# DeltaNet and channel mixer on one core: one block substitution for both units of batch 0, with a new order of the work

## The chip, the cores and the metric

The program runs on one core of one Trainium2 chip. Its time is the device time of one launch in microseconds (us); the kernel before takes 618.48 us, the median of 3 runs (618.42 to 619.09). A core has five engines with queues of their own: TensorE (PE, with its weight loads shown as PEld), VectorE (DVE), ScalarE (ACT), GpSimd (POOL) and SyncE (SP). Each works through its queue in the order in which the program emitted it, and semaphores make an instruction wait for another engine.

## The reference

Four batches, eight heads, 768 tokens, 48 channels per head; then a channel mixer over 384 channels with a low-rank token mix of rank 32.

```python
def _attn_ref(q, k, v, beta) -> np.ndarray:
    B, H, S, D = q.shape
    k_n = k / (np.linalg.norm(k, axis=-1, keepdims=True) + 1e-06)
    state = np.zeros((B, H, D, D), dtype=np.float32)
    y = np.zeros_like(q)
    for t in range(S):
        kt, vt, bt = (k_n[:, :, t], v[:, :, t], beta[:, :, t, None])
        y[:, :, t] = np.einsum('bhd,bhde->bhe', q[:, :, t], state)
        v_old = np.einsum('bhde,bhd->bhe', state, kt)
        state = state + bt[:, :, :, None] * np.einsum('bhd,bhe->bhde', kt, vt - v_old)
    return y.astype(np.float32)
...
def _moe_ref(x, U, V, w_ch1, w_ch2) -> np.ndarray:
    xt = x.transpose(0, 2, 1)
    h = xt @ U @ V
    u = x + h.transpose(0, 2, 1)
    ch = np.maximum(u @ w_ch1, 0.0) @ w_ch2
    return (u + ch).astype(np.float32)
```

The weights `U`, `V`, `w_ch1` and `w_ch2` arrive as 64-bit floats and are turned into 32-bit ones on the chip, in integer and float operations.

## The kernel before

**The recurrence in chunks.** Each batch's 768 tokens are cut into 12 chunks of 64. Six chunks of all eight heads form a unit, so there are eight units, two to a batch (`SPLIT = (0, 1)` are those of batch 0). For each unit the kernel

1. loads k, q, v and a second copy of k (`load`, L513; names "k", "q", "v", "z") over SP's and POOL's queues;
2. transposes k and q on TensorE (`turn`, L646 or L420, copied out by ScalarE at L660 or, for the first, L655 and L657) and multiplies them in `products` (L673). The 32 x 32 diagonal blocks of the k products go to `diag` (ScalarE L683, VectorE L686), the whole to `pg` (L693), for units 0 and 1 also to half of `hs` (`alone`, L697); the q products are masked into `qk` by VectorE (L704);
3. lays the diagonal blocks out for VectorE in `gs`, one block per partition, by a 32 x 32 transpose (L749), takes the norms of k from their diagonals (`norms`, L593 to L618) and puts the factor beta/norm^2 on the diagonal of `xt`, which POOL has zeroed (L743);
4. inverts the triangular blocks by substitution: VectorE scales `gs` (L753) and then does one multiplication (L758, into `prod`) and one subtraction (L764, into `xt`) per step. For units 0 to 2 each 32 x 32 block is taken as two 16 x 16 blocks side by side (15 steps), for the others whole (31 steps);
5. transposes the result back into `zz` (L771), joins the 16 x 16 halves on TensorE where a unit was split (`joins`, L780 to L837, with `part` at L790 writing to `S1` and `S2`), and the 32 x 32 blocks into 64 x 64 ones (L854 to L885); `diagonals` (L893, L900) puts the blocks in place in `pg`.

There is one `gs`, one `xt` and one `zz`. So unit n is laid out when unit n-1 is substituted, and returned to `zz` when unit n-1 is joined.

**The recurrence.** `recur` runs over the 12 chunks of a batch. `prepare` (L973, L984, copied out at L992 and L997) makes ready three chunks at a time from a joined half of a unit. Each chunk then needs a product with the state (L1022), a subtraction on VectorE (L1035), the state's update (L1050, added at L1060) and the outputs (L937, L951), which ScalarE copies to `X` (L921).

**The weights.** `load_weights` fetches 14 slices: 0 is U, 1 is V, 2 to 7 are `w_ch1`, 8 to 13 are `w_ch2`. Each is converted by VectorE in five operations (L1155 to L1183), with one of ScalarE (L1140) between. The slices land in three rooms in turn: the half of `X` that batch 1 uses later, `wide`, and the first half of `hs`.

**The mixer.** `front` does the low-rank token mix and transposes its result into `ut` (L1346 to L1390), 256 tokens at a time, three groups to a batch. `channels` is the first layer (L1447, six pairs of tiles for each group, with ReLU at L1412), `narrow` the second (L1562), done with seven products on sums and differences of halves (`add_up`, `sums`); VectorE adds its results to `X` (L1487). Batch 3 uses such sums for its first layer too (`quick`, L1251). `channels`, `narrow`, `front` and `turn` have a second form in which a product is split into quarters of the array (L408, L420); it is taken while other quartered work is running, where the list of places allows it with the word `quad`.

**What sets the order.** The work is written as generators, and a planner in the program (`run`, L341) interleaves them before anything runs on the chip. Each yield is a need (keys that other parts have emitted) or an operation with engine and assumed cost. Of the operations that could start about as soon, the one with the lowest rank goes first. Ranks come from the list `PLACES` (L142 to L258), by name of the part and its indices; a part that isn't listed has the default given at `begin`. The planner only fixes the order in each engine's queue; the waits between engines follow from which tile is written and read where.

Of the kernel before, what the change touches and what calls it, by code (L numbers as in the profile page):

```python
# [8 lines left out]
FP32 = mybir.dt.float32  # L9
# [7 lines left out]
BK = 32  # L17
# [9 lines left out]
def kernel(  # L27
# [115 lines left out]
    add_up b0 i0 76.06; add_up b0 i1 10; add_up b0 i2 92; add_up b1 i0 94.5; add_up b1 i1 -57.95  # L143
    add_up b1 i2 13.5; add_up b2 i0 4.89; add_up b3 i0 119.12; add_up b3 i1 17.69; add_up b3 i2 2.95
    blocks n1 83.63; blocks n2 19.95; blocks n3 96.74; blocks n4 107.02; blocks n5 204.56; blocks n6 121.16
    blocks n7 126.66; both 73; channels b0 i0 e0 96.95; channels b0 i0 e1 105.6; channels b0 i0 e2 -27.57
    channels b0 i0 e3 129.38; channels b0 i0 e4 91.95; channels b0 i0 e5 71.15; channels b0 i1 e0 25
    channels b0 i1 e1 19.03; channels b0 i1 e2 34; channels b0 i1 e3 5.2; channels b0 i1 e4 84.16
    channels b0 i1 e5 30.5; channels b0 i2 e0 52; channels b0 i2 e1 46.94; channels b0 i2 e2 75.56
    channels b0 i2 e3 116.36; channels b0 i2 e4 51.09; channels b0 i2 e5 99.28; channels b1 i0 e0 113.65  # L150
    channels b1 i0 e1 91.5; channels b1 i0 e2 53.98; channels b1 i0 e3 100.61; channels b1 i0 e5 120.34
    channels b1 i1 e0 128.05; channels b1 i1 e1 30.85; channels b1 i1 e2 104.15; channels b1 i1 e3 58.65
    channels b1 i1 e4 15.5; channels b1 i1 e5 91.65; channels b1 i2 e0 118.43; channels b1 i2 e1 -2.08
    channels b1 i2 e2 73.28; channels b1 i2 e3 -8.98; channels b1 i2 e4 111.65; channels b1 i2 e5 32.87
    channels b2 i0 e0 38.24; channels b2 i0 e2 4.5; channels b2 i0 e3 127.92; channels b2 i0 e4 22.75
    channels b2 i0 e5 95.78; channels b2 i1 e0 274.53; channels b2 i1 e1 94; channels b2 i1 e2 97.16
    channels b2 i1 e3 91.59; channels b2 i1 e4 73; channels b2 i1 e5 1.09; channels b2 i2 e0 28.09
    channels b2 i2 e1 44.19; channels b2 i2 e2 57.06; channels b2 i2 e3 68.5; channels b2 i2 e4 73
    channels b2 i2 e5 9.5; copies 56.49; cut 75.73; diagonals n0 h0 19.22; diagonals n0 h1 62.5
    diagonals n1 h0 52; diagonals n2 h0 15.5; diagonals n2 h1 94.5; diagonals n3 h0 32; diagonals n3 h1 93.24  # L160
    diagonals n4 h0 7.5; diagonals n4 h1 95.58; diagonals n5 h0 33.96; diagonals n5 h1 27; diagonals n6 h0 92.63
    diagonals n6 h1 -0.5; diagonals n7 h0 88.94; diagonals n7 h1 69.62; first 30.4; front b0 i0 -7.49
    front b0 i0 quad 1; front b0 i1 75.5; front b0 i1 quad 1; front b0 i2 -10.38; front b1 i0 71.77
    front b1 i1 76; front b1 i1 quad 1; front b1 i2 73.06; front b2 i0 4.43; front b2 i0 quad 1; front b2 i1 12.82
    front b2 i1 quad 1; front b2 i2 68.32; front b2 i2 quad 1; front b3 i1 -1.47; front b3 i2 94.5
    gather b0 i0 h0 c0 77.72; gather b0 i0 h0 c1 16.74; gather b0 i0 h1 c0 -15; gather b0 i1 h0 c0 -18.11
    gather b0 i1 h0 c1 -19.16; gather b0 i1 h1 c0 111.34; gather b0 i1 h1 c1 99.53; gather b0 i2 h0 c0 109.5
    gather b0 i2 h0 c1 36.92; gather b0 i2 h1 c0 4.78; gather b0 i2 h1 c1 84.78; gather b1 i0 h0 c0 21.21
    gather b1 i0 h1 c0 79.5; gather b1 i0 h1 c1 103.91; gather b1 i1 h0 c0 92.5; gather b1 i1 h0 c1 122.8
    gather b1 i1 h1 c0 101.5; gather b1 i2 h1 c0 77.08; gather b1 i2 h1 c1 45; gather b2 i0 h0 c0 13.32  # L170
    gather b2 i0 h0 c1 82.99; gather b2 i0 h1 c0 124.83; gather b2 i0 h1 c1 3.53; gather b2 i1 h0 c0 80.62
    gather b2 i1 h0 c1 73.95; gather b2 i1 h1 c0 80.36; gather b2 i1 h1 c1 76.58; gather b2 i2 h0 c0 95.84
    gather b2 i2 h1 c0 25.35; gather b3 i0 h0 c0 2.88; gather b3 i0 h0 c1 113; gather b3 i0 h1 c1 113
    gather b3 i1 h0 c0 -4; gather b3 i1 h0 c1 23.12; gather b3 i1 h1 c0 44.69; gather b3 i1 h1 c1 28.1
    gather b3 i2 h0 c0 105.1; gather b3 i2 h0 c1 37.88; gather b3 i2 h1 c0 109.03; gather b3 i2 h1 c1 92.38
    grams n0 i0 54.5; grams n0 i1 5; grams n1 i0 -5.73; grams n1 i1 16.5; grams n2 i0 64.85; grams n2 i1 5.5
    grams n3 i0 10.25; grams n4 i0 140.55; grams n4 i1 0; grams n6 i1 103.46; grams n7 i0 120.26
    grams n7 i1 124.04; joins n0 h1 42; joins n1 h0 -10.78; joins n1 h1 90.6; joins n2 h0 46.2; joins n2 h1 -9.38
    joins n3 h0 18.36; joins n3 h1 -3; joins n4 h0 49.57; joins n4 h1 108.36; joins n5 h0 6.33; joins n5 h1 -4.95
    joins n6 h1 102.05; joins n7 h0 91.09; joins n7 h1 -26.22; last_sum b0 i0 107.65; last_sum b0 i1 -0.5  # L180
    last_sum b0 i2 58; last_sum b1 i0 6.24; last_sum b1 i1 90.99; last_sum b1 i2 72.32; last_sum b2 i0 -3.27
    last_sum b2 i1 94.5; last_sum b3 i1 76.04; last_sum b3 i2 90; load n0 namek halves(0,) -2.13
    load n0 namek halves(1,) 6.19; load n0 nameq halves(0,) 89.12; load n0 nameq halves(1,) 77.79
    load n0 namev halves(0,) 106; load n0 namez halves(0,) 113.97; load n0 namez halves(1,) 7.5
    load n1 namek halves(0,) 81.07; load n1 namek halves(1,) 73.91; load n1 nameq halves(0,) 43.57
    load n1 nameq halves(1,) 91.1; load n1 namev halves(0,) 27.89; load n1 namev halves(1,) 70.76
    load n1 namez halves(0,) 93.39; load n1 namez halves(1,) 5.01; load n2 namek halves(0, 1) 29.55
    load n2 nameq halves(0, 1) 67.61; load n2 namev halves(0, 1) 60.56; load n2 namez halves(0, 1) 107.23
    load n3 namek halves(0, 1) 11; load n3 nameq halves(0, 1) -4.84; load n3 namev halves(0, 1) 66.59
    load n3 namez halves(0, 1) 25.89; load n4 namek halves(0, 1) 65.35; load n4 nameq halves(0, 1) 24.5  # L190
    load n4 namev halves(0, 1) 81; load n4 namez halves(0, 1) 30.74; load n5 namek halves(0, 1) 109.5
    load n5 nameq halves(0, 1) 92; load n5 namev halves(0, 1) 38.85; load n5 namez halves(0, 1) -21.49
    load n6 namek halves(0, 1) 32.5; load n6 nameq halves(0, 1) 37.61; load n6 namev halves(0, 1) 7.15
# [388 lines left out]
    def landed(name, n, j=1):  # L582
        return need(*[(name, n, g, j) for g in range(2)])

    def norms(n):

        _, _, _, _, _, vn, _, _ = units[n]
        b, hf = divmod(n, NU)
# [1052 lines left out]
```

## Time and profile before

| what | value |
| --- | --- |
| median of 3 runs | 618.48 us (618.42 to 619.09) |
| span of the profiled execution | 612.3 us |
| PE busy | 582.1 us (95%) |
| PEld busy | 502.3 us (82%) |
| DVE busy | 417.3 us (68%) in 1000 instructions |
| ACT busy | 236.6 us (39%) |
| POOL busy | 98.4 us (16%) |
| first L1447 (first layer of the mixer) | 119.84 us |
| first L1562 (second layer) | 143.0 us |
| shares of the chain that ended last | PE 83%, DVE 11%, issue 2%, ACT 2% |

The span counts from the first to the last instruction of one profiled execution; the runs are timed from outside it, so their median is 6.2 us longer. Busy times are those of the engine's own instructions, without waits. A stretch's clock is the share of full speed that TensorE was granted in it.

### The profile page before, as it was taken

To read this page: it belongs to the slowest core of one execution; us is meant where nothing else is said; L and a number is where in the kernel's file an instruction comes from. 1 tells how busy PE (TensorE), PEld (TensorE's weight loads), DVE (VectorE), ACT (ScalarE), POOL (GpSimd) and SP (SyncE) were. 2 spreads that over 40 slices of the span, in tenths; PEclk is the share of its full clock that TensorE was granted. 3 is DMA by queue.
4 is the path that set the end of the run, shared out by engine and by line. 5 is a ranking of instruction groups with operands and counts; after the bars stand their busy time and mean duration, and the time that the engine had idled before them with its cause. 6 is when DMAs were issued, how large, how long until landed. Compare 5 with 4: busy or idle time off the path is not lost.

```text
span 612.3 us, 24053 instructions
## 1 busy us (share of the span) xinstructions
PE 582.1 (95%) x10824; PEld 502.3 (82%) x10824; DVE 417.3 (68%) x1000; ACT 236.6 (39%) x466; POOL 98.4 (16%) x169
## 2 busy tenths in 40 slices
PE   4798887999999999999999999999999999999997
PEld 4788786688989987988889988978989889656997
DVE  5998899898899348988895888287843223332542
ACT  3645666255412652265218224253163220344000
POOL 8321050520004304110043002220010000000000
PEclk9655557799999999999999999999999999999999
DMA  9911686940006205200071002310000000000000
GB/s 142 163 42 55 209 193 169 137 130 19 3 28 98 67 4 91 61 16 3 4 123 42 16 16 53 74 42 4 28 3 3 29 2 1 26 2 0 16 36 27
DMA packets 63847, 33.31 MB, mean 54 GB/s; under 512 B 50816, under 2 KB 61824, under 8 KB 63744
## 3 DMA queue, kind: packets, MB, share of 16 engines
q1 hardware_dynamic: 56800, 23.21, 17.6%
q0 software_dynamic: 5344, 8.27, 6.5%
q8 instruction: 85, 1.39, 0.9%
q10 hardware_dynamic: 1600, 0.30, 0.3%
q14 instruction: 18, 0.15, 0.1%
HBM read 27.03 MB, written 4.72 MB: 52 GB/s over the span
## 4 chain that ended last, share of the span: by engine, by line
PE 83%; DVE 11%; issue 2%; ACT 2%; POOL 1%; DMA 1%; DVEq 0%; ACTq 0%; POOLq 0%
PE P L1562 25%; PE P L1447 24%; PE P L1251 7%; PE P L673 3%; PE P L408 3%; PE P L1364 2%; PE P L646 2%; PE P L1022 2%; PE P L973 2%; PE P L1050 2%; PE P L984 2%; PE P L951 2%; DVE prod L758 2%; PE P L937 2%; DVE xt L764 2%
## 5 line engine op out<-in xcount | busy, mean ns | idle before, releaser
L1447 PE MATMUL P<-ut,w_sb 128*128 128x256 f32 x648 | 151.6, 385 | 0.1
L1447 PEld LDWEIGHTS P<-ut,w_sb 128*128 128x128 f32 x648 | 119.4, 190 | 18.2 <-issue 1.2
L1562 PE MATMUL P<-w_sb,hs 128*128 128x192 f32 x468 | 82.4, 330 | 0.2 <-ACT hs L1412 0.2
L1562 PEld LDWEIGHTS P<-w_sb,hs 128*128 128x128 f32 x468 | 75.9, 190 | 2.0 <-ACT hs L1412 0.3
L764 DVE TENSOR_TENSOR xt<-xt,prod 128x112 f32<-128x112 f32 (+21 forms) x200 | 64.6, 323 | 6.9
L758 DVE TENSOR_TENSOR prod<-gs,xt 128x112 f32<-128x112 f32 (+21 forms) x200 | 64.0, 320 | 4.4
L1487 DVE TENSOR_TENSOR X<-X,P 128x192 f32<-128x192 f32 x84 | 29.3, 351 | 53.5 <-PE P L1562 50.7
L1412 ACT ACTIVATE hs<-P 128x512 f32<-128x512 f32 x54 | 32.3, 597 | 82.9 <-PE P L1447 73.6
L921 ACT COPY X<-P 64x192 f32<-64x192 f32 x96 | 30.0, 313 | 80.7 <-PE P L951 74.0
L1562 PE MATMUL P<-w_sb,S 128*128 128x192 f32 x264 | 45.9, 328 | 0.0
L1562 PEld LDWEIGHTS P<-w_sb,S 128*128 128x128 f32 x264 | 42.9, 190 | 1.2 <-DVE X L1487 0.6
L531 POOL DMA_DIRECT2D slot<-in_k_dram x44 | 29.1, 671 | 64.3 <-PE P L1050 64.2
L646 PE MATMUL P<-ident,slot 128*128 128x128 f32 x192 | 30.8, 309 | 8.2 <-DMA slot<-in_k_dram 8.1
L673 PE MATMUL P<-slot 48*64 48x64 f32 x1536 | 32.8, 243 | 4.8 <-ACT slot L660 4.8
L893 ACT COPY slot<-zz 32x384 f32<-32x384 f32 x64 | 32.5, 508 | 9.1 <-DVE zz L832 4.9
L673 PEld LDWEIGHTS P<-slot 48*64 48x64 f32 x1536 | 29.4, 155 | 7.9 <-ACT slot L660 6.0
L646 PEld LDWEIGHTS P<-ident,slot 128*128 128x128 f32 x192 | 25.0, 158 | 11.7 <-issue 8.7
L1251 PE MATMUL P<-slot,w_sb 128*128 128x384 f32 x96 | 33.2, 486 | 0.0
L1562 PE MATMUL P<-w_sb,slot 128*128 128x192 f32 x180 | 30.6, 327 | 0.9 <-DVE X L1487 0.9
L660 ACT COPY slot<-P 128x768 f32<-128x768 f32 x30 | 23.5, 796 | 20.1 <-PE P L646 18.0
L1562 PEld LDWEIGHTS P<-w_sb,slot 128*128 128x128 f32 x180 | 29.4, 190 | 2.0 <-DVE X L1487 1.5
L531 POOL DMA_DIRECT2D slot<-in_q_dram x32 | 21.0, 664 | 56.8 <-ACT X L921 40.5
(150 smaller groups left out, 935.9 us busy)
## 6 DMA issues: line engine op xcount, KB each, us to landing
out_dram<-X SPq DMA_DIRECT2D x22, 192.0 KB, 1.9
X<-in_moe_w_ch_dram SPq DMA_DIRECT2D x10, 384.0 KB, 3.9
wide<-in_moe_w_ch_dram SPq DMA_DIRECT2D x10, 384.0 KB, 4.4
slot<-in_k_dram SPq DMA_DIRECT2D x48, 72.0 KB, 4.8
slot<-in_k_dram POOLq DMA_DIRECT2D x44, 72.0 KB, 4.8
slot<-in_q_dram SPq DMA_DIRECT2D x32, 72.0 KB, 4.4
slot<-in_q_dram POOLq DMA_DIRECT2D x32, 72.0 KB, 4.7
slot<-in_v_dram SPq DMA_DIRECT2D x32, 72.0 KB, 3.4
```

Source lines behind the costliest of these rows:

```text
L531: queue.dma_start(out=t[half(1 - g if name == "z" else g), :, to, 0:D], in_=src[b, 4 * g + s, hf * UC * L : (hf + 1) * UC * L, :].rearrang ...
L646: nc.tensor.transpose(p_t[:, c // 3, c % 3], t[:, c, 2 * j : 2 * j + 2].rearrange("p s d -> p (s d)"), ident,)
L673: nc.tensor.matmul(p_g[half(g ^ (par * i)), par, c], kq[rows, c, j, 0, half(g)], kq[rows, c, j, i, half(g)], start=True, stop=True,)
L758: nc.vector.tensor_tensor(out=prod, in0=gb[:, :, j : j + 1, j + 1 :].to_broadcast([128, split, m, w]), in1=xb[:, :, 0:m, j : j + 1].to_bro ...
L764: nc.vector.tensor_tensor(out=xb[:, :, 0:m, j + 1 :], in0=xb[:, :, 0:m, j + 1 :], in1=prod, op=ALU.subtract,)
L893: nc.scalar.copy(pg[quarter(i), :, at, :, a : a + BK], cut(zc, h)[quarter(i)].rearrange("p r (c j) t -> p r c j t", j=2),)
L921: nc.scalar.copy(x[half(c % 2), c // 2, 4 * D * g : 4 * D * (g + 1)].rearrange("p (j r d) -> p r j d", r=2, d=D), states(p_y)[half(g)],)
L1251: nc.tensor.matmul(to, w, t, start=start, stop=stop, skip_group_check=True)
L1412: nc.scalar.activation(hs[:, fs[0] : fs[1] + 1 : fs[1] - fs[0]], p_f, ACTF.Relu)
L1447: nc.tensor.matmul(p_f[:, x], w(x, t), ut[:, t], start=(t == 0), stop=(t == KT - 1))
L1487: nc.vector.tensor_tensor(out=to, in0=to, in1=p, op=ALU.add)
L1562: nc.tensor.matmul(to, of[0], of[1], start=of[2], stop=of[3], skip_group_check=True)
```

## The change

Units 0 and 1 no longer take turns in `gs`, `xt` and `zz`. Each gets its own matrices in `w2_sb`, the room of the second layer's weights, which is filled later: `matrices` returns, for units 0 and 1, a part of `gs_first`, of `xt_first` and of the rest of that room; the other units keep the old tiles. One substitution then runs over both, with the four 16 x 16 blocks of a partition (two per unit) in each operation: 15 steps for both units in place of 15 each. The norms of both are taken together as 64 columns, and POOL zeroes both matrices in one instruction. `blocks` is cut into `lay`, `substitution`, `back` and `rest`; `lay` and `back` are parts with ranks of their own.

```diff
+    def matrices(n):
+
+        if n in SPLIT:
+            at = slice(MS * n, MS * n + MS)
+            return gs_first[:, at], xt_first[:, at], first[:, 4 * MS :][:, ZZ * n : ZZ * n + ZZ]
+        return gs.rearrange("p s t -> p (s t)"), xt.rearrange("p s t -> p (s t)"), zz
...
+    def norms(n, many=1):
...
+        yield need(("seeded", n), ("scaled", n - 2), *[("laid", n + y) for y in range(many)])
...
+    def lay(n):
+        diag = units[n][6]
+        yield need(*[("diag", n, j) for j in range(2)], *[("substituted", n - 1)] * (n >= NU))
         yield op("dve", 2.0)
+        nc.vector.transpose(squares(matrices(n)[0]), diag.rearrange("p q t -> p t q"))
+        emitted(("laid", n))
+
+    def back(n):
+        yield need(("substituted", n), *[("joined", n - 1)] * (n > NU))
+        yield op("dve", 2.0)
+        _, x, z = matrices(n)
         nc.vector.transpose(
+            z[:, 0 : BK * BK].rearrange("p (q t) -> p t q", t=BK),
+            squares(x).rearrange("p s t -> p t s"),
         )
         emitted(("returned", n), 0.1)
+        yield from rest(n)
+
+    def first_blocks():
+
+        def seed():
+            yield op("pool", 2.1)
+            nc.gpsimd.memset(xt_first, 0.0)
+            emitted(("seeded", 0), 0.1)
+
+        begin(seed(), place_of(0))
+        for n in SPLIT:
+            begin(lay(n), place_of(n))
+        yield need(("c", 0))
+        yield from substitution(
+            diagonal_blocks(gs_first, 4), diagonal_blocks(xt_first, 4), factors(slice(0, 2), 4), 4
+        )
+        for n in SPLIT:
+            emitted(("substituted", n))
+            begin(back(n), place_of(n))
```

Since the rooms are shared with other data, the planner gets further needs. Weight slices 8 to 13 go into `w2_sb` and are converted after both units are joined. Unit 1's `part` writes to the two tiles of `ut`, which are now fixed tiles, where unit 0's keeps `S1` and `S2`. Loads of a unit wait for the last use of the unit two before; batch 0's copies to `X` wait for beta's second half, batch 1's for the last weight slice; the ReLU of batch 0 waits for slice 7, which lands in `hs`.

```diff
-            yield need(("wide", i))
+            yield need(("wide", i), *[("joined", y) for y in range(NU)] * (i >= W2))
...
+        es_area = (S1, S2) if n == 0 else ut_sb
...
-        yield need(("rec", n - 2), *[("x", b - 1, UC * hf + c) for c in range(UC)])
+        yield need(("rec", n - 2), ("used", n - 2), *[("x", b - 1, UC * hf + c) for c in range(UC)])
...
+        yield need(("betas", 0)) if u else []
...
-            yield need(("stored", b - 2, c // 2)) if b > 1 else []
+            yield need(("stored", b - 2, c // 2)) if b > 1 else need((("beta", 1), ("weights", W2 + 5))[b])
...
+            yield need(("freed", W2 - 1)) if b == 0 else []
```

The list `PLACES` is a new one: of its 511 entries 19 are the same in the new list, which has 625. `quad` stands at 33 of the 54 groups of `channels` (before at none), at 19 of `narrow` (18), 16 of `turn` (13) and 7 of `front` (6). Two of its lines, before and after:

```diff
-    turn n3 i0 j0 namek quad 1; turn n3 i0 j1 namek 100.4; turn n3 i1 j0 nameq 51.57; turn n3 i1 j1 nameq 105.5
...
+    turn n3 i0 j1 namek quad 1; turn n3 i1 j0 nameq 115.16; turn n3 i1 j0 nameq quad 1; turn n3 i1 j1 nameq 117.39
```

## The prediction

> **What bounds the kernel now.** I read four views: busy time in slices, the same by stretches, VectorE's timeline, and the chain of waits. First the slices (tenths of 15.3 us each; PEclk is the granted TensorE clock).
>
> ```profile
> PE   4798887999999999999999999999999999999997
> DVE  5998899898899348988895888287843223332542
> PEclk9655557799999999999999999999999999999999
> ```
>
> There are two stages. Up to about 126 us TensorE runs at a low clock while VectorE is full; after it TensorE is full at full clock. By stretches (us; busy PE, PEld, DVE, ACT, POOL with instruction counts; clock, DMA share, GB/s):
>
> ```profile
> 13.70:30.00 16.30, 11.96 (x253) 10.39 (x252) 14.95 (x45) 12.28 (x24) 6.22 (x11) 0.69 1.01 167
> 30.00:58.00 28.00, 24.56 (x776) 22.83 (x773) 25.09 (x70) 13.31 (x29) 5.27 (x10) 0.55 0.20 54
> 80.00:110.00 30.00, 24.20 (x793) 20.93 (x789) 28.51 (x55) 19.24 (x38) 11.42 (x18) 0.67 0.75 173
> 126.00:200.00 74.00, 73.97 (x1445) 65.58 (x1434) 67.22 (x147) 29.33 (x55) 11.35 (x19) 1.00 0.27 58
> ```
>
> VectorE is busy 14.95 of 16.30 and 25.09 of 28.00 us (the rest is mostly 0.03 us between instructions), TensorE 73.97 of 74 from 126 us on. So the end is the length of the head plus a nearly fixed amount of TensorE work, and the head is as long as VectorE's queue. That queue's timeline (start, duration, operation) shows what the change touches:
>
> ```profile
> 17.19 0.69 DVE L753 TENSOR_TENSOR gs<-gs,cp 128x512 f32<-128x512 f32 x1
> 22.43 0.28 DVE L758 TENSOR_TENSOR prod<-gs,xt 128x128 f32<-128x128 f32 x1
> 24.24 0.73 DVE L686 SCALAR_TENSOR_TENSOR slot<-P,even,slot 128x192 f32<-128x192 f32 x2
> 27.64 2.05 DVE L771 STREAM_TRANSPOSE zz<-xt 128x1024 f32<-128x1024 f32 x1
> 32.62 1.91 DVE L749 STREAM_TRANSPOSE gs<-slot 128x1024 f32<-128x1024 f32 x1
> 37.91 0.69 DVE L753 TENSOR_TENSOR gs<-gs,cp 128x512 f32<-128x512 f32 x1
> 55.63 2.07 DVE L771 STREAM_TRANSPOSE zz<-xt 128x1024 f32<-128x1024 f32 x1
> ```
>
> Unit 0 is substituted from 17.19 to 27.64, unit 1 from 37.91 on. Unit 1's diagonal blocks are complete at 24.97 (the L686 pair); they are laid into gs only at 32.62, after unit 0 is done with it.
>
> **The substitution.** Unit 0 takes 0.72 us for the scaling (17.19 to 17.91) and 9.73 for 30 operations up to 27.64, of which the two L686 pairs between them take 0.65 and 0.66: 8.42. Together 9.14, for two units 18.28. After, step j works on 4(j+1)(15-j) elements: 60, 112, 156, 192, 220, 240, 252, 256 and back. Units 3 to 7 have operations of just these sizes (groups by form, from 160 us on: count, busy us, mean ns):
>
> ```profile
> L753 DVE TENSOR_TENSOR gs<-gs,cp 128x1024 f32<-128x1024 f32 x5 | 6.1, 1211 | 0.0
> L764 DVE TENSOR_TENSOR xt<-xt,prod 128x60 f32<-128x60 f32 x10 | 2.2, 222 | 0.3
> L764 DVE TENSOR_TENSOR xt<-xt,prod 128x256 f32<-128x256 f32 x5 | 2.1, 425 | 0.2
> ```
>
> With the rows of all eight sizes, for both lines, the 30 operations sum to 10.37 us; starts lie 0.03 further apart than durations (0.46 against 0.42 at 256), so 11.33, and with the scaling 1.21 it is 12.54. **Saved: 5.74 us** of VectorE. Blocks in one operation cost nothing by themselves: two blocks of 63 (128x126) take 290 ns, one row of 135 takes 297.
>
> **The norms.** Five small operations from 15.97 to 17.19, 1.22 us per unit, become one set of 64 columns. Their rows exist at 32 columns only. Bounds for the set: 1.37 (five times the 0.03 that 30 more elements cost at L758) to 1.72 (the reciprocal, 0.35, doubled as well); I take 1.55, since the reciprocal is the one far above the others' 0.19. Saved 0.9. One transpose of the rows instead of two of 0.20: 0.15. VectorE's ledger: 5.74 + 0.9 + 0.15 = **6.8 us saved**.
>
> **The new wait.** The joint substitution needs unit 1's blocks, so it can't start at 17.19. They were there at 24.97, behind unit 0's copies on ScalarE (L693, L697); placed first, the same steps from the end of unit 1's transposes at 17.08 sum to 0.78 (L660) + 1.56 (L673) + 0.58 (L683) + 0.73 (L686) + some 0.5 between engines: 21.3. Behind either come 1.9 for laying, 0.5 for the square root and 1.55 for the norms: start at 25.3 to 28.9. In VectorE's in-order queue everything emitted behind it waits too: unit 0's return at L771, hence its joins, ScalarE's copies of them and the recurrence. From 13.7 to that start VectorE has, of work that is in the ledger anyway, the laying of both units 3.7, unit 1's L686 pairs 1.4, two transposes of beta 0.6 and the norms 1.55: 7.2 us; up to 3.5 more may be drawn forward (the masks of unit 0's products L704, 2.0; the first weight slice, 1.5). Idle: 11.6 - 7.2 - 3.5 = 0.9 at best, 15.2 - 7.2 = 8.0 at worst. I take **3.5**: unit 1's k early, but some of the filling missing, as 50 to 60 us also shows it when data come late (8.66 busy of 10).
>
> **Moved and added at nothing.** One zeroing on POOL of twice the size (2 x 1.0 us) stands 1 us longer ahead of POOL's later loads; unit 0's q products ran at 26 to 28 us, some way behind. Weight slices 8 to 13 go into the room of the first matrices and wait for both units' joins; before, those ended at 87.3 (L881) and slice 8 began at 92.95, a cover of 5.6 us that unit 1's earlier end widens; without it each slice late costs 3.98 (L1155 to L1183: 0.56, 0.55, 0.96, 0.95, 0.96). ReLU of batch 0 waits for slice 7 (90.7 against 123 needed). The recurrence of batch 1 writes X only after all slices: 149 against 159.2, a cover of 10. Loads of unit 2 wait for unit 0's last state product, 81.15 against 82.14 now. With nothing of these on the path the head gets 6.8 - 3.5 = **3.3 us shorter** (from 5.9 shorter to 1.2 longer).
>
> **The new order.** It is drawn anew everywhere, so the TensorE part moves too. There a group of six L1447 takes 1.30 us behind its like and 1.49 behind another shape: 0.19 per change of shape. The list of ranks now lets 33 of the 54 first-layer groups run split in quarters, none before, and so skip the change. Net eight changes fewer make 1.5 us; by 20 more or fewer it would be 4 either way. I take **-1.5**.
>
> Sum: 612.3 - 3.3 - 1.5 = 607.5 of span. The median lies 6.2 above that execution's span, so **613.7**.
>
> **Rivals.** *Faster still: the recurrence is the limit.* The chain of waits (start, duration) has TensorE, not VectorE, here:
>
> ```profile
> 56.47 1.31 PE P L973 x48
> 57.85 2.60 PE P L814 x45
> 60.60 1.33 PE P L984 x36
> 61.93 2.49 PE P L828 x45
> ```
>
> Unit 1's joins stand in the middle of batch 0's recurrence at a clock of 0.50. Done together and earlier, they leave a denser stretch, and the clock rises sooner: 16 L1022 take 0.68 at half clock (82.87) and 0.45 where it is up (75.61), 16 L1050 0.57 (103.22) against 0.36 (93.74). Over 11 and 10 of these groups that is 11 x 0.23 + 10 x 0.21 = 4.6, giving 609.1 where VectorE's queue leaves room for it. Against it: VectorE is full to 110 us.
> The Trainium skill, "TensorE: Matmul & The Clock Gate", Part 1, has it that a busy window of about 3.4 us brings the full clock and an idle one halves it. The trace doesn't fit that simply: from 40 to 70 us TensorE is busy over 8.8 of each 10 us and the clock stays 0.50.
>
> *Slower: unit 0's late start is carried through.* Its substitution ends at 25.3 + 12.5 = 37.8 instead of 27.64. Some 5 us of the 20.4 that followed until the first products were ready (48.0) were unit 1's laying, norms and masks, which now lie ahead; so the recurrence starts 5 us later, and if its 59 us (48 to 107) keep their length, 612.3 + 5 + 6.2 = 623.5. It decides if the steps of the recurrence, not the weight conversions between them, fill VectorE's queue. For it: everything behind hangs on that recurrence. Against it: in those 59 us it stood from 56.5 to 64.5 and 66.8 to 75.6 for halves that would be ready earlier.
>
> *Slower: the order costs more in the TensorE part* than the head gains, 20 changes of shape more (3.8) and the head as at the poor end (+1.2): 623.5 again; milder mixes end near 620.
>
> *No change: the saving goes into waiting* (idle 6.8 instead of 3.5, order neutral), or the parts are not merged in effect because unit 1 comes at 28.9: 618.5.
>
> **Chances.** Forecast 0.40, faster still 0.21, no change 0.09, late start 0.18, poor order 0.12. Some 0.2% (1.2 us) is what a measurement of this kernel can tell from no change; so faster 0.61, same 0.09, slower 0.30. The forecast's own range is 608.6 to 617; reaching into the rivals on both sides, 605.5 to 623.5 leaves out about 2 in 10.
>
> **What would show it.** Operations L758 and L764 of the first units: 30 instead of 60, up to 0.42 us each, between about 26 and 39 us; VectorE's idle between 13.7 and their start (3.5 forecast; over 7 speaks for no gain); the return of unit 1 near 42 instead of 55.63; the first L1447 at 116 to 117 instead of 119.84; TensorE full behind it and the stretch from the first L1447 to the end 492.5 us long now, 491 after. The forecast is wrong if the first L1447 comes later than 120, or if that stretch differs by more than 4.

## The result and the profile after

The changed kernel takes 621.17 us (median of 9 runs, 619.25 to 623.13) against 618.37 for the kernel before on the same chip: a ratio of 1.0068 (95% interval 1.0046 to 1.0090). Set against each other once more, on another chip, they give 621.68 against 618.63, 1.0053 (1.0024 to 1.0083). The quotients of these medians are 1.0045 and 1.0049. It is slower by half a per cent, where 613.7 was forecast.

One thing about the profile shown before has to be said first. Around every later execution of either kernel 1.7 us lie outside the span. The execution shown, with its span of 612.3, was therefore one of about 614 us, among the quickest of its kernel (614.15 is the lowest of some 100 runs). Another profiled execution of the same kernel has a span of 621.3. The same stretches of the two, first the one shown, then the other (us; busy PE, PEld, DVE, ACT, POOL; clock, DMA share, GB/s), up to the first L1447, behind it, and 90 to 100 us:

```profile
13.70:119.84 106.14, 89.82 (x2508) 78.56 (x2507) 97.17 (x225) 61.49 (x120) 30.83 (x50) 0.63 0.65 142
119.84:612.30 492.46, 485.28 (x8183) 417.55 (x8181) 313.59 (x748) 171.44 (x340) 55.41 (x93) 1.00 0.15 33
90.00:100.00 10.00, 6.21 (x231) 5.17 (x224) 9.93 (x18) 6.81 (x13) 1.29 (x3) 0.97 0.92 211
```

```profile
13.70:124.76 111.06, 92.82 (x2518) 81.34 (x2517) 98.10 (x227) 61.80 (x120) 31.01 (x50) 0.62 0.65 136
124.76:621.30 496.54, 487.68 (x8183) 419.11 (x8181) 313.64 (x748) 171.94 (x340) 55.48 (x93) 1.00 0.15 33
90.00:100.00 10.00, 6.66 (x179) 5.95 (x182) 6.90 (x12) 4.63 (x7) 2.16 (x4) 0.50 1.04 184
```

One program, and the first L1447 comes 4.9 us later. Two things differ ahead of it. TensorE was granted 0.50 instead of 0.97 of its clock from 90 to 100 us; and between 87 and 99 us it stood still twice within a group of products, for 1.25 and 2.46 us, where the execution shown before has two such stops of 0.16 and 0.20 us (the last section returns to them). VectorE, "full" in the execution that the forecast rests on, was busy for 6.90 of these 10 us. A single profile of this kernel is good to some 4 us, so what follows goes by medians, ratios and several profiles.

The changed kernel in slices, then the stretch behind its first L1546 and the stretches shown of before:

```profile
PE   5669895999999999999999999999999999999997
DVE  5788987799989898426889888349862225332542
PEclk9665655799999999999999999999999999999999
```

```profile
122.70:621.20 498.50, 488.76 (x9104) 415.28 (x9104) 315.38 (x771) 173.75 (x360) 57.70 (x97) 1.00 0.14 31
13.70:30.00 16.30, 10.77 (x254) 9.74 (x254) 13.22 (x30) 10.74 (x22) 4.74 (x8) 0.72 1.04 179
30.00:58.00 28.00, 22.94 (x631) 21.89 (x629) 24.55 (x48) 13.93 (x26) 6.76 (x12) 0.56 0.21 46
80.00:110.00 30.00, 20.98 (x756) 19.11 (x758) 23.90 (x44) 14.26 (x30) 11.51 (x19) 0.56 0.73 146
126.00:200.00 74.00, 73.31 (x1834) 63.04 (x1832) 67.36 (x171) 28.57 (x58) 13.02 (x21) 1.00 0.19 38
```

The two stages are still there. The first L1546 (before L1447) comes at 122.70, in a second execution at 121.97. From 80 to 110 us VectorE has idle time, and the stretch from the first L1546 to the end is 498.5 us long (second execution 498.0). VectorE's timeline shows the change itself (start, duration, operation, idle time before it and what ended that):

```profile
23.39 0.19 DVE L639 TENSOR_SCALAR norm<-norm 128x64 f32<-128x64 f32 x1
24.89 1.22 DVE L772 TENSOR_TENSOR w_sb<-w_sb,cp 128x1024 f32<-128x1024 f32 x1
32.23 0.42 DVE L777 TENSOR_TENSOR prod<-w_sb 128x256 f32<-128x256 f32 x1
38.49 2.01 DVE L812 STREAM_TRANSPOSE w_sb<-w_sb 128x1024 f32<-128x1024 f32 x1
42.40 2.04 DVE L812 STREAM_TRANSPOSE w_sb<-w_sb 128x1024 f32<-128x1024 f32 x1
...
104.98 0.35 DVE L1129 TENSOR_TENSOR z<-slot,P 128x192 f32<-128x192 f32 x1
107.24 0.73 DVE L1253 TENSOR_SCALAR power<-wide 128x768 int32<-128x768 int32 x1 [1.91 <-DMA wide<-in_moe_w_ch_dram]
107.90 0.73 DVE L1259 TENSOR_SCALAR X<-wide 128x768 int32<-128x768 int32 x1
108.55 0.33 DVE L1156 TENSOR_TENSOR s<-s,P 128x192 f32<-128x192 f32 x1
110.55 0.34 DVE L1129 TENSOR_TENSOR z<-slot,P 128x192 f32<-128x192 f32 x1
...
115.87 0.56 DVE L1450 COPY tt<-P 128x384 f32<-128x384 f32 x1 [4.11 <-PE P L1444]
```

Up to 42 us all goes as forecast: norms 1.50, then 13.60 to the return, of which 0.93 is another pair of operations, so 12.67 for the substitution. Unit 1 is back at 42.40 (before 55.63), unit 0 at 38.49 (before 27.64). Behind the dots the saving is gone: VectorE, an in-order queue, stands at L1253 until 107.24 for a weight slice, with the recurrence's s (L1156) queued behind it, and later waits 4.11 us for TensorE. Between 13.7 us and the first layer VectorE is busy 91.0 and 90.2 us in the two executions, against 97.2 and 98.1 before. That is about the saving (the two heads don't hold quite the same work: the old one has most of unit 2's substitution, the new one three more weight slices), and 18.0 and 18.1 us idle against 9.0 and 13.0 is where it went. Over the whole run VectorE is busy 412.9 and 412.6 us against 417.3 and 417.9, in 36 instructions fewer; with the 0.03 us between two instructions that makes 5.5 to 6.4 us saved.

### The profile page after: what moved, and what is told of

It is laid out like the page before. It is cut to its first block, busy times and chain, and to the rows that moved or that the text cites. A ratio compares the mean times of both kernels' runs of the same rounds, so it can differ in the third digit from the quotient of the medians.

```text
span 621.2 us, 25811 instructions
## 1 busy us (share of the span) xinstructions
PE 582.5 (94%) x11724; PEld 498.9 (80%) x11724; DVE 412.9 (66%) x964; ACT 238.6 (38%) x483; POOL 97.7 (16%) x168
## 4 chain that ended last, share of the span: by engine, by line
PE 84%; DVE 6%; ACT 4%; DMA 3%; issue 2%; SPq 1%; DVEq 0%; ACTq 0%
PE P L1661 25%; PE P L1546 15%; PE P L434 11%; PE P L1349 7%; PE P L723 3%; PE P L1462 2%; PE P L696 2%; DMA wide<-in_moe_w_ch_dram 2%; PE P L1067 2%; PE P L1116 2%; PE P L1045 2%; PE P L1078 2%; PE P L922 2%; PE P L1031 2%; PE P L908 1%
## 5 line engine op out<-in xcount | busy, mean ns | idle before, releaser
L1546 PE MATMUL P<-ut,w_sb 128*128 128x256 f32 x420 | 98.1, 385 | 0.6 <-DVE X L1586 0.3
L1661 PE MATMUL P<-w_sb,hs 128*128 128x192 f32 x504 | 88.6, 330 | 0.7 <-issue 0.6
L1546 PEld LDWEIGHTS P<-ut,w_sb 128*128 128x128 f32 x420 | 77.5, 190 | 11.9 <-DVE X L1586 0.5
L1661 PEld LDWEIGHTS P<-w_sb,hs 128*128 128x128 f32 x504 | 81.8, 190 | 4.5 <-issue 1.6
L1586 DVE TENSOR_TENSOR X<-X,P 128x192 f32<-128x192 f32 x85 | 29.7, 352 | 67.4 <-PE P L1661 59.3
L434 PE MATMUL P<-ut,w_sb 64*64 64x256 f32 x912 | 60.8, 383 | 2.8 <-ACT hs L1511 2.6
L1511 ACT ACTIVATE hs<-P 128x512 f32<-128x512 f32 x54 | 32.3, 598 | 78.1 <-PE P L1546 54.2
L783 DVE TENSOR_TENSOR xt<-xt,prod 128x31 f32<-128x31 f32 (+20 forms) x170 | 57.0, 335 | 5.8
L777 DVE TENSOR_TENSOR prod<-gs,xt 128x31 f32<-128x31 f32 (+20 forms) x170 | 56.5, 332 | 3.6
L569 POOL DMA_DIRECT2D slot<-in_k_dram x44 | 28.9, 665 | 83.9 <-PE P L1144 83.7
L434 PEld LDWEIGHTS P<-ut,w_sb 64*64 64x64 f32 x912 | 31.5, 133 | 13.1 <-ACT hs L1511 4.3
L1661 PE MATMUL P<-w_sb,S 128*128 128x192 f32 x240 | 41.4, 328 | 0.0
L994 POOL MEMSET slot<- 32x384 f32 x32 | 13.4, 418 | 128.6 <-PE P L951 89.3
```

Of the source, the lines that this page charges most:

```text
L434: nc.tensor.matmul(to[half(g)], w[half(r), half(g)], x[half(r)], start=start, stop=stop, skip_group_check=True,)
L569: queue.dma_start(out=t[half(1 - g if name == "z" else g), :, to, 0:D], in_=src[b, 4 * g + s, hf * UC * L : (hf + 1) * UC * L, :].rearrang ...
L777: nc.vector.tensor_tensor(out=prod, in0=gb[:, :, j : j + 1, j + 1 :].to_broadcast([128, split, m, w]), in1=xb[:, :, 0:m, j : j + 1].to_bro ...
L783: nc.vector.tensor_tensor(out=xb[:, :, 0:m, j + 1 :], in0=xb[:, :, 0:m, j + 1 :], in1=prod, op=ALU.subtract,)
L1511: nc.scalar.activation(hs[:, fs[0] : fs[1] + 1 : fs[1] - fs[0]], p_f, ACTF.Relu)
L1546: nc.tensor.matmul(p_f[:, x], w(x, t), ut[:, t], start=(t == 0), stop=(t == KT - 1))
```

## The experiments

Theory A is the forecast's: the head (all up to the first layer) is as long as VectorE's queue. Theory B: the head follows unit 0's later return. Theory C: the new order costs more in the TensorE part. D and E came up on the way. Except for the two unaltered kernels, the runs below play back a recorded order of instructions, so that an edit moves nothing but what it names; `apart`, `in_turn` and `in_step` had to be given orders of their own near the changed kernel's. Ratios are to the kernel before, run on the same chip, where its median was 617.66 to 619.93 us; they differ from the quotients of the medians by up to 0.2%.

| run | median us | ratio (95% interval) | first layer at | from there to the end |
|---|---|---|---|---|
| before, again (one execution) | 622.98 | - | 124.76 | 496.5 |
| changed, again | 621.68 | 1.0053 (1.0024-1.0083) | 121.97 | 498.0 |
| after_full | 622.09 | 1.0058 (1.0035-1.0081) | 123.13 | 498.5 |
| after_late | 625.81 | 1.0110 (1.0081-1.0139) | 125.05 | 498.3 |
| before_full | 623.73 | 1.0068 (1.0044-1.0091) | 120.74 | 501.2 |
| before_late | 623.86 | 1.0096 (1.0057-1.0136) | 126.93 | 494.2 |
| before_full97 | 623.51 | 1.0110 (1.0077-1.0143) | 126.35 | 495.4 |
| lighter | 621.81 | 1.0044 (1.0007-1.0081) | 119.40 | 498.2 |
| before_lighter | 620.31 | 1.0029 (0.9992-1.0066) | 122.33 | 495.0 |
| in_turn | 624.95 | 1.0095 (1.0064-1.0126) | 125.83 | 499.0 |
| in_step | 628.53 | 1.0150 (1.0104-1.0196) | 127.97 | 498.5 |
| apart | 623.76 | 1.0120 (1.0080-1.0160) | 124.81 | 498.1 |
| slice_behind | 620.96 | 1.0025 (1.0002-1.0047) | 120.70 | 498.6 |
| two_moves | 619.49 | 1.0022 (0.9993-1.0050) | 119.84 | 498.6 |
| unit2_early | 620.66 | 1.0021 (1.0005-1.0036) | 119.59 | 497.8 |
| plain_channels | 632.99 | 1.0220 (1.0170-1.0271) | 119.62 | 510.4 |
| after_half_joins | 625.85 | 1.0131 (1.0096-1.0166) | 121.64 | 500.2 |
| before_half_joins | 623.36 | 1.0079 (1.0050-1.0107) | 122.41 | 503.6 |

The last two columns are of one execution each.

**The originals again.** 

> The kernel before, profiled once more, as a baseline taken beside the experiments. No theory is at stake in its time (618 to 619); its stretches are wanted: first L1447, and first L1447 to the end (119.84 and 492.5 in the execution shown, whose span was 612.3).

 

> The changed kernel, unaltered, on the same chip as the next two runs, to set them against: 621 to 622.

 The baseline's stretches turned out 4.9 and 4.1 us longer than in the execution shown, the changed kernel's 0.7 and 0.5 shorter.

**Work added to VectorE, in several places.**

```diff
+        nc.vector.memset(gs, 0.0), four times (before: a spare 128x256, fifteen times)
# after_full: behind weight slice 11; after_late: before the joint scaling
# before_full: behind slice 10; before_full97: behind slice 8; before_late: before unit 0's scaling
```

> The changed kernel, its instruction order fixed, with four extra zeroings of 128x1056 (some 4 us of VectorE in all) behind the last step of weight slice 11, where its timeline shows VectorE idle for 4.11 us until L1444. Theory A (the forecast's: the head is as long as VectorE's queue): the end moves by the whole added work, 621 to about 625. Theory B (what was saved has turned into waiting for a recurrence that starts late): the work falls into that hole and the end stays within 1 us of 621. Theory C (the new order in the TensorE part is to blame) says nothing of it.

 

> The changed kernel with the same four zeroings right before the joint scaling at L772, so that the substitution of both units starts some 4 us later. Theory A: the same 4 us as when they stand behind slice 11, about 625. Theory B: here they delay unit 0's return and so the recurrence, 624 to 625, and this place costs at least 2.5 us more than the place behind slice 11.

 

> The kernel before, its order fixed, with fifteen zeroings of 128x256 (4 to 5 us of VectorE in all) behind the last step of weight slice 10, at 97 us, where VectorE has no idle time. Theory A: the end moves by all of it, 618.4 to 622.5 or 623.5. Theory B agrees for this kernel, since unit 2 already stands in VectorE's queue there: 621 to 623.5.

 

> The kernel before with the same fifteen zeroings right before unit 0's scaling at L753 (17 us). Theory A: 622.5 to 623.5, as behind slice 10. Theory B: the same, as long as the recurrence has VectorE work to wait behind at every place; less if the start of the recurrence has slack in this kernel.

 

> The kernel before with the fifteen zeroings (5.75 us of VectorE in the trace of the run that had them at 130 us) behind slice 8 counted from 0, which ends at 97.0. In the two executions profiled, VectorE is idle between 85 and 112 for 0.9 and for 4.6 us. Theory A and B: VectorE's queue is full here, 618.6 + 4 to 5.75, so 622.5 to 624.5. If it costs less than 2, the kernel before has the same slack as the changed one, and the comparison of the two holes shows nothing.

In after_full the four stand in the hole in front of L1450:

```profile
112.23 0.94 DVE L1284 MEMSET gs<- 128x1056 f32 x1 [0.17 <-issue]
...
115.90 0.94 DVE L1284 MEMSET gs<- 128x1056 f32 x1 [0.29 <-DVE gs L1284]
116.76 0.49 DVE L1450 COPY tt<-P 128x384 f32<-128x384 f32 x1
```

4.6 us of VectorE work cost 0.4 to 0.9 there (622.09 against 621.68 and 621.17), within what the ratios can tell from nothing. The same work ahead of the substitution costs 4. Slices are counted from 0, so the one called 10 in before_full's expectation ends at 130.0 and not at 97; its zeroings stood from 130.1 to 135.8, where the first layer has begun. before_full97 has them at 98.6. In the kernel before the 5.75 us cost 5.1 at 130, 5.2 at 17 and 5.9 at 98 us. So this kernel has no hole at any of these places, and the changed one has: theory A, by which added VectorE work lengthens the head wherever it stands, does not hold of the changed kernel.

**Work taken from VectorE.**

```diff
-            nc.vector.scalar_tensor_tensor(
+            if i not in (1, 2, 3): nc.vector.scalar_tensor_tensor(
                 out=power, in0=h, scalar=-(1 << 31), in1=power,
```

> The changed kernel, its order fixed, without the L1271 step of the slices of V and of the first two first-layer slices: these three slices keep no signs. That takes 3 x 0.95 = 2.85 us out of VectorE's queue at 55.8, 61.0 and 66.0, ahead of the first state copy at 68.47. Theory A: the head gets 2.85 us shorter, 618.4. Theory B (there the joins of both units on TensorE at half clock set the start of the recurrence): the first state copy stays within 1 us of 68.5, and the end within 1 of the changed kernel.

 

> The kernel before without the L1173 step of the slices of V and of the first two first-layer slices (these keep no signs): 3 x 0.95 = 2.85 us less for VectorE between 54 and 72, the same cut that left the changed kernel where it was (621.8 against 621.7). Theory A and B: here VectorE's queue is the head, so 615.5 to 616.5. If it stays at 618, a saving of VectorE work of this size shows in neither kernel, and the forecast's assumption was wrong of the kernel before as well.

 621.81 against 621.68, and 620.31 against 617.66: no gain in either. In lighter's profile the first state copy stays at 67.7 (67.4 in the changed kernel's second execution), as B had it, but the first layer comes 2.6 us earlier, as A had it; the ten times, spread from 617.8 to 625.5, don't confirm the profile. What is sure is that the kernel before is not simply as long as its VectorE queue either: work added to it costs all of itself, work taken from 54 to 72 us brings nothing, since another chain is next.

**The merging alone.**

```diff
-        yield from substitution(
-            diagonal_blocks(gs_first, 4), diagonal_blocks(xt_first, 4), factors(slice(0, 2), 4), 4
-        )
         for n in SPLIT:
+            yield from substitution(*[diagonal_blocks(x, 2) for x in matrices(n)[:2]], factors(slice(n, n + 1), 2), 2)
             emitted(("substituted", n))
             begin(back(n), place_of(n))
# in_turn: unit 0's return and first joins ahead of unit 1's steps; in_step: behind them
```

> The changed kernel with the merging undone but all else kept (own rooms, joint norms, ranks): after the joint norms unit 0's two blocks are substituted with operations of two blocks, unit 0 returns and its joins start, then unit 1's two blocks. VectorE gets back the 5.7 us that merging saved, but unit 0's substitution ends 24.9 + 9.1 = 34.0 instead of 38.5. Theory A (the head is as long as VectorE's queue): 5 to 6 us slower than the changed kernel, 626 to 627, and equal to the next run. Theory B (what counts is when unit 0 comes back, since its joins on TensorE run beside unit 1's substitution): the time stays at 618 to 622 although VectorE does 5.7 us more.

 

> The same kernel and the same operations of two blocks each, but unit 1's substitution stands ahead of unit 0's return, so that both units come back together as in the changed kernel, at about 24.9 + 18.3 = 43. Theory A: equal to the run in which the units take turns. Theory B: at least 4 us slower than that run (unit 0 returns 9 us later), 625 to 629.

 By the ratios merging is worth 0.8 to 1.0% against in_step (5 to 6 us, the 5.7 of the forecast), where both units return together as in the changed kernel, and 0.3 to 0.4% (some 2) against in_turn. Between these two, with equal work, unit 0's return at 36.2 instead of 43.3 is worth 3.4 us (1.0150 - 1.0095), half a microsecond for one (the two orders had to differ in more places than this return, so the share of the return alone is not shown). So both are true: VectorE's work ahead of unit 0's return is on the path, and unit 0's lateness eats a part of it. Theory A's "equal" fails, theory B's 618 to 622 too.

**Units apart, unit 0 early.**

```diff
-            if n not in SPLIT:
-                begin(norms(n), place_of(n))
-            elif n == 0:
-                begin(norms(0, NU), place_of(0))
+            begin(norms(n), place_of(n))
# the same for blocks(n)
```

> The changed kernel's rooms, ranks and TensorE part, but norms and substitutions of units 0 and 1 apart, as before, and unit 0's chain ranked ahead: its substitution at about 17 to 20, its return at about 30 instead of 38.5, with unit 1's substitution behind it, beside unit 0's joins. VectorE gets the 6.8 us of work back that the merging saved. Theory A (queue): the same VectorE work as in the run with the units in turn, which took 625.0, so 625 again. Theory B (unit 0's return): unit 0 is 4 to 6 us earlier than there, which at the 0.4 to 1 us per us seen so far gives 619 to 623; not slower than the changed kernel in spite of 6.8 us more VectorE work.

 Unit 0 is back at 31.7, the recurrence starts at 61.4 instead of in_turn's 73.4 and ends at 113.4 instead of 114.3. Twelve microseconds of earlier start are worth one, and the ratio is no better than in_turn's. A late recurrence as the cause by itself, theory B, falls with this run: its end hangs on what is done beside it. Nothing is merged here and the kernel is 1.0% (by the medians) to 1.2% slower than before, so the rooms and the order of this run cost more than the merging brings.

**Moves on VectorE.** slice_behind (two_moves: the first hunk too):

```diff
-L1253, L1259, L1265, L1271, L1281 (slice of U, at 21 us)
 L639 ... L772
...
 L874 (unit 1's first joins)
+L1253, L1259, L1265, L1271, L1281 (slice of U)
...
-L1253, L1259 (slice 11)
 L1156 s
-L1265, L1271 (slice 11)
 L1129 z
+L1253, L1259, L1265, L1271 (slice 11)
 L1281 (slice 11)
```

> The changed kernel, its order fixed, with one move on VectorE: the first four steps of weight slice 11 (L1253 to L1271) stand behind the recurrence's last s and z (L1156, L1129) instead of ahead of them. Its first step waits until 107.24 for a transfer of 9.71 us, while the products that the recurrence waits for are older. Theory B with the late transfer as part of it: the recurrence's end comes some 2.5 us earlier (110.55 to about 108), the front L1444 and the first L1546 follow by 1.5 to 2.5, and the end is at 619 to 620. Theory A (VectorE's work is the same): no change, 621. Theory C (TensorE part): no change.

 

> The changed kernel, its order fixed, with two moves on VectorE and no change of work: the steps of weight slice 11 behind the recurrence's last s and z, as before, and the conversion of U's slice (five operations from 21.33 to 23.39, 1.5 us) behind unit 1's first joins transpose at 44.48, where VectorE waited 1.46 us for L922. Theory A (the length of VectorE's queue): no change. Theory B (lateness of unit 0, then of the recurrence's end): the substitution starts 0.6 to 1.5 us earlier and the first L1546 comes 2.5 to 3 us earlier, some 120; end 618.5 to 619.5, level with the kernel before.

 Without a change of work 0.3 to 0.4% come back: 619.49 against 621.68 on one chip, 2.2 us. In slice_behind the recurrence's last steps now wait for TensorE only:

```profile
104.72 0.35 DVE L1156 TENSOR_TENSOR s<-s,P 128x192 f32<-128x192 f32 x1 [0.87 <-PE P L1144]
108.67 0.35 DVE L1129 TENSOR_TENSOR z<-slot,P 128x192 f32<-128x192 f32 x1 [3.59 <-PE P L1116]
108.94 0.55 DVE L1253 TENSOR_SCALAR power<-wide 128x768 int32<-128x768 int32 x1
```

The last z comes at 108.67 instead of 110.55, the first L1546 at 120.70. So some 2 us of the loss were VectorE's queue standing at a slice whose transfer was late. The chain of waits of the changed kernel names that transfer (start, duration):

```profile
95.82 0.95 DVE power L1271
96.77 0.27 DVE s L1156
97.04 0.32 SPq L1230
97.36 0.04 issue
97.40 9.71 DMA wide<-in_moe_w_ch_dram
```

It runs beside unit 2's loads, which start at 90.7 us here and started at 82 to 83 before: they wait for unit 0's last product.

**Quarters undone.** The diff is in the order alone: the 19 first-layer parts that took the quartered form take the whole one.

> The changed kernel, its order fixed, with the 19 first-layer parts that it runs in quarters (38 groups) run whole again. Theory C (the quarters cost more than the changes of shape that they save): by the trace a whole L1546 takes 0.233 us, four quarters of L434 4 x 0.0667 = 0.267, so 228 products get 7.6 us cheaper; this order then has 75 more changes of shape at 0.19, 14 us. Taken together 621 + 14 - 8 = 627. If quarters cost nothing by themselves, as the forecast had it: 621 + 14 = 635. If changes of shape don't cost 0.19 here: below 621.

 The stretch from the first layer on grows by 12 us, close to the 14 of "quarters cost nothing". In the changed kernel's groups (from 126 us on: count, busy us, mean ns):

```profile
L1546 PE MATMUL P<-ut,w_sb 128*128 128x256 f32 x414 | 96.5, 385 | 0.5 <-DVE X L1586 0.3
L434 PE MATMUL P<-ut,w_sb 64*64 64x256 f32 x912 | 60.8, 383 | 2.8 <-ACT hs L1511 2.6
```

96.5 / 414 = 0.233 us for a whole product, 4 x 60.8 / 912 = 0.267 for one in quarters: 228 of them cost 7.6 more, and 2.6 us of waiting for the ReLU (L1511), which the kernel before does not have. Counted in the traces from 126 us on, plain_channels has some 73 changes of shape more than the changed kernel, and the kernel before some 27 more (one or two more or less, by what is taken for one shape): 73 changes less 10.2 make the 12, so a change costs 0.30 by this estimate, not 0.19. Quarters pay in this order, and against the old order, by the same estimate, they pay nothing: 10.2 - 27 x 0.30 = +2.1.

**Work taken from TensorE.**

```diff
-                    for rows in map(half, range(2)) if lone else map(quarter, range(4)):
+                    for rows in () if n == 1 and y % 2 else map(half, range(2)) if lone else map(quarter, range(4)):
```

> The changed kernel, its order fixed, with half of unit 1's join products on TensorE left out (every second of L908 and L922). A group of 48 takes 2.75 us there at half clock, unit 1 has four: 5.5 us less TensorE work between 53 and 78, and none less on VectorE. Theory D (new: from 40 to 90 us TensorE at half clock sets the pace, 9 to 10 of 10 us busy, so VectorE work saved there turns into waiting): 3 to 5.5 us faster than the changed kernel, 616 to 618.5. Theory A (VectorE's queue): no change, 621.5. Theory B (unit 0's return alone): no change, since unit 1's joins are behind it.

 

> The kernel before with the same half of unit 1's joins left out (every second of L814 and L828; they stand at 57.85 and 61.93 in its chain of waits, and later). Theory D: 2 to 5 us faster than the kernel before, although removing 2.85 us of VectorE work at 54 to 72 brought nothing. Theory A: no change.

 Both got slower, by 0.6 to 0.8%. The runs settle nothing about theory D, since leaving TensorE's instructions out moved something else: TensorE stands still in the middle of groups where the profile names nothing that it waits for ("issue"; see the last section). From 126 us on this sums to 6.8 us in before_half_joins, 1.3 and 3.1 in the two executions of the kernel before. Whether TensorE at half clock sets the pace from 40 to 90 us stays open.

**Unit 2 earlier on TensorE.**

```diff
 L1144 x8
+L696 x6 (unit 2's first turn)
 L1031 x8
 L1116 x8
+L723 x24 (its products)
 L1045 x16
-L696 x6
 L1444 x6
```

> The changed kernel with the two moves of the run before (slice 11 behind the recurrence, U's slice behind unit 1's first transpose) and, on TensorE, unit 2's first turn (L696) and products (L723) inside the recurrence's last steps instead of behind them, its second turn behind the front's first product; ScalarE's and VectorE's copies of them follow. No work is added or left out. In the kernel before, unit 2's first turn stands at 92 to 94 us, in the changed one at 111.5, behind the whole recurrence, though TensorE is busy for 5 of 10 us from 100 to 110 there. Theory E (new: the 3 to 4 us that the stretch behind the first L1546 is longer are work of unit 2 that the old order did inside the recurrence): the front starts 1.5 us earlier, the first L1546 comes at 117 to 119 with as much of unit 2 done as before it, and the end is 1 to 3 us below the 619.5 of the run with two moves, 616.5 to 618.5. Theory A (VectorE's queue): 619.5, as with the two moves, since VectorE's work is the same.

 The front starts at 108.79 instead of 110.91, then waits for copies to `X` on ScalarE, and the first L1546 comes at 119.59 instead of 119.84. The ratio is that of two_moves. As many turns and products lie ahead of the first layer as in two_moves, so the run shows only that this place is not what delays the front; it doesn't show what the stretch behind would gain from more of them. No version beats the kernel before.

## Why the prediction was wrong

It said 613.7, faster; it is 621.2, slower. The cost of the operations held; two other steps failed. The term for the new order was off by about 5 us, and the head, whose moved parts were costed at nothing, by about 2.

**Right.** Substitution 12.54 (measured 12.67), norms 1.55 (1.50), a start at 25.3 to 28.9 (24.89, just ahead of that range), idle time before it 3.5, between 0.9 and 8.0 (1.82 + 0.29), unit 1's return near 42 (42.40), 6.8 us of VectorE work saved (5.5 to 6.4).

**The new order, "I take -1.5".** This is the larger error. Of the stretch from the first layer to the end, five profiles of kernels with the old order and nothing added there have 492.5 to 496.5, mean 494.7 (before_half_joins, which leaves products out, is not among them); eleven with the new order, plain_channels and after_half_joins aside, have 497.8 to 499.0, mean 498.4. That is +3.7, whatever the head did, 5.2 off. The forecast counted changes of shape and took quarters for free. It also took the work of this stretch as fixed. Counted in the traces, 13 turns, 12 groups of products and 8 of the front's products with V (L1364) lie ahead of the first layer in the kernel before; in the changed one it is 12, 10 and 4 (L1462). One turn at 0.87, two groups at 0.86 and four products at 0.35 are 4.0 us of TensorE work that went from the head into the stretch in which TensorE is full. Unit 2's first turn now stands behind the whole recurrence; before, it stood inside it (at 92.43 us, and at 94.19 in the other execution). Two lines of before and two of after:

```profile
92.43 0.87 PE L646 MATMUL P<-ident,slot 128*128 128x128 f32 x6
113.75 1.81 PE L1364 MATMUL P<-tt,v_sb 128*128 128x384 f32 x4
```

```profile
111.55 1.54 PE L696 MATMUL P<-ident,slot 128*128 128x128 f32 x6
124.09 1.45 PE L1462 MATMUL P<-tt,v_sb 128*128 128x384 f32 x4
```

With quarters and shapes (+2.1) that is 6.1, 2.4 more than measured. So the size of the step is measured, and its parts are an estimate that no run tried one by one; the rest of the new order may have saved the 2.4.

**"With nothing of these on the path the head gets 3.3 us shorter".** The first layer comes at 122.7, 122.0 and 123.1 (after_full) against 119.8, 124.8 and 120.7 (before_full): no shorter. (The medians, less 1.7 and less the mean stretch behind, give 121.1 and 121.6 against 122.0.) Two of the things costed at nothing came onto the path. "Loads of unit 2 wait for unit 0's last state product, 81.15 against 82.14 now": that product came later with unit 0, the loads began at 90.7 and ran beside the weight slices, whose cover was said to widen (that the loads made slice 11 late was not tried); VectorE's queue then stood at slice 11 ahead of the recurrence. With the order mended (two_moves) the first layer comes at 119.8 and the time falls by 2.2. Then 619.5 less the stretch's 3.7 would be 615.8, and the head is 2.8 us shorter than before, near the forecast's 3.3. But 4.0 us of TensorE work had left that head too, so how much of the 2.8 is the merging's is not shown.

**"The head is as long as VectorE's queue".** It holds for work added to the kernel before, and for work ahead of unit 0's return (the merging). It does not hold for the hole at 112 us, nor for work taken from 54 to 72 us in either kernel. The view behind it, VectorE at 28.51 of 30 us, was of a quick execution; the next one had 25.38.

**The rivals.** "The order costs more in the TensorE part" (0.12) is nearest: the right place, by other means than changes of shape, which became fewer. "Unit 0's late start is carried through" (0.18) had the right sign: a start at 29.2 instead of 24.6 costs 3.7 (after_late against after_full). But it priced a recurrence of constant length, and that one shrank from some 55 us (51.2 to 106.1) to 42 (68.5 to 110.5); in apart an early start brought nothing. "Faster still" (0.21) wanted a clock that rises sooner; it is 0.56 from 80 to 110, against 0.67 and 0.50 in the two executions of the kernel before. The Trainium skill, "TensorE: Matmul & The Clock Gate", Part 1, would have the full clock follow a busy window of some 3.4 us; from 50 to 60 us TensorE is busy over 10.00 of 10 at 0.50, so the trace does not agree.

**The 6.2 us** between span and median were 1.7 around the span and 4.5 because that execution was quick. The sum's baseline was right by this, but not the picture that it was read from.

## What to carry to other kernels

A change that saves work on one engine and comes with a new order is two changes: cost the order by which work changes sides (here 4.0 us of TensorE work that used to hide in the head), not only by its seams. "Full" in a profile means that added work costs, not that removed work pays; ask which chain is next, and what is queued in order behind the first late transfer. Before building on a single profile, set its span against the median: one that lies well below the others shows a kernel busier than it usually is.

## What the runs showed of the hardware that was not expected

The same program's first layer began at 119.8 or 124.8 us with the granted clock from 90 to 100 us at 0.97 or 0.50. And TensorE stops in the middle of groups of like products, for up to 3.6 us, where the profile names nothing that it waits for. In two_moves twice behind the eleventh of sixteen:

```profile
97.68 0.66 PE L1116 MATMUL P<-s,slot 48*64 48x48 f32 x11 [0.63 <-DVE s L1156]
100.39 0.35 PE L1116 MATMUL P<-s,slot 48*64 48x48 f32 x3 [2.04 <-issue]
104.88 0.66 PE L1031 MATMUL P<-s,slot 48*64 48x48 f32 x11 [0.53 <-DVE s L1156]
107.40 0.35 PE L1031 MATMUL P<-s,slot 48*64 48x48 f32 x3 [1.87 <-issue]
```

From 60 to 126 us such stops sum to 1.0 and 4.4 us in the two executions of the kernel before, 4.0 and 3.3 in the changed one's, 6.7 in two_moves. Their places and lengths differ from execution to execution and from kernel to kernel, by as much as the effects looked for here.

The kept traces do say what they come with. In the twenty of them, 52 stops of half a microsecond or more lie inside a group later than 57 us. Every one ends 1.2 to 1.8 us after a packet of 16 KB has landed on the DMA queue that carries instructions, although from 57 to 130 us these packets land 3.4 to 10.6 us apart. That fits a TensorE that has run out of instructions until the next packet is in. It would also fit the two runs that left products out and became slower, as fewer instructions shift where the packets begin and end. No run changed when these packets are loaded, so the cause is not shown.
